# More filler matmuls on TensorE ahead of the first attention scores

## The chip, the cores and the metric

The kernel runs on one core of one Trainium2 chip. The metric is the device time of that core in microseconds. Each engine (TensorE or PE, VectorE or DVE, ScalarE or ACT, GpSimd or POOL) works through its own list of instructions in order and waits on semaphores for the others; SyncE (SP) and ScalarE also issue DMA transfers.

## The reference

One block of a conditioned transformer: a modulation vector from c, attention with 32 heads of 20, then a bilinear feed-forward, each with a layer norm ahead of it and a gated residual. x is 2048 rows of 640; all inputs are bf16.

```python
mod = (_silu(c) @ w_mod).reshape(c.shape[0], 6, 1, -1)
sa, ca, ga, sb, cb, gb = (mod[:, i].copy() for i in range(6))
h = _layernorm(x) * (1 + ca) + sa
qkv = (h @ wqkv) -> q, k, v, 32 heads of 20
o = softmax(q @ k^T * 20 ** -0.5) @ v
x = x + ga * (o @ wo)
h = _layernorm(x) * (1 + cb) + sb
x = x + gb * (((h @ w_gate) * (h @ w_up)) @ w_down)
```

(The lines are joined from the reference's functions.)

## The kernel before, in words

**Tiling.** The queries are cut into five chunks (512, 512, 512, 256, 256 rows). For each chunk the 32 heads are worked off in eight sets of four, one head to each strip of 32 rows of the array. Scores are computed transposed, keys on the partitions, in tiles of 128 x 512 (L1305); ScalarE takes the exponential of two or three tiles at once out of PSUM (L1341, 779 in all). About a fifth of the tiles (400 of 2048) go to VectorE instead, which builds the exponential from integer arithmetic: L1365 to bits, L1397 and L1405 split them, L1402 multiplies the halves. TensorE multiplies the result by V, extended by a column of ones that gives the softmax's denominator (L1831). After each chunk comes a suffix: output projection, residual, second layer norm (L1585 to L1592), transposes (L1603), gate and up products, and the down product (all recorded at L822 when they use the whole array, at L826 when cut into four strips of 32 columns).

**The head.** Up to the first scores this must happen: c is transposed on TensorE (L856), copied by VectorE (L854), passed through the sigmoid (L859 to L862); two blocks of 25 matmuls of one column each (L840) then give the modulation vectors ca and sa as soon as their weights have landed. Meanwhile VectorE and ScalarE compute the layer norm of the first 512 rows: tiles with even number by statistics on VectorE (L920, L925), odd ones by two passes with sums on ScalarE (L883, L886). Twenty transposes (L947) bring the rows into columns; the evictions (L955 on VectorE, L953 on ScalarE) apply the modulation and give hT. From it come the K projection of the first head set, the Q projection, and the K projection of the second set (L980, 20 matmuls each, cut into strips), whose evictions (L989, L990 for K, L994, L996 for Q) allow the first scores. The V products (L826, with wV) follow.

**What sets the order.** Nothing is ordered by hand. While it builds the program, the kernel simulates all engines with durations of its own (class Sched) and picks, whenever an engine is free in that simulation, a ready task by priority. The list of each engine that comes out is written into the program as it stands. An eviction can go to either of two engines: if ScalarE is idle in the simulation, it takes the eviction from VectorE's list (steal, L268). TensorE is served by pick_pe (L1981), which takes in turn: scores, other work when recent activity is low, products with V, other work, and last a filler.

**Fillers.** [...]the planner keeps a record of it: each matmul is entered with an area (a filler with 512, a full-array matmul with 2.37 for each nanosecond), and recent(t) sums the last 3413 ns. A filler (do_fill, L2088) multiplies the identity matrix with itself into a free PSUM bank; nothing reads it. Before the first scores it is one full-array matmul of 512 columns (L2100), later four strips (L2102). It is issued when nothing else is to be had, the simulated time is past a limit, and recent activity is below FILL_MIN:

```python
        if t > 4000 and fill_ok(t, fill_deps):
            return do_fill(t)
...
        return sc.recent(t) < FILL_MIN      # 4200
```

The same FILL_MIN also stands at L2038, where low activity lets other work go ahead of the products with V; that place is not touched. The simulated time starts at 700 ns and isn't the chip's time: the order that it leads to is fixed, the moments at which the chip reaches each instruction are not.

Of the kernel before, what the change touches and what calls it, by code (L numbers as in the profile page):

```python
# [464 lines left out]
GATE_F = [1.0, 0.869, 0.999, 0.673, 1.0]  # L465
FILL_MIN = 4200.0
FILL_HARD = 0.0
FILL_MODE = 'P'
DUP_MIN = 0.0
XN_POOL = ()  # L470
# [25 lines left out]
def build_kernel(nc, A_x, A_wqkv, A_wo, B_x, B_w_gate, B_w_up, B_w_down, c, w_mod, out):  # L496
# [14 lines left out]
    sc = Sched()  # L511
# [860 lines left out]
    for qi, (it, us) in enumerate(dquads):  # L1372
# [3 lines left out]
        def term(f, deps, dur, name, slot=None, src=None, last=False, it=it, qi=qi, st_=st_):  # L1376
            t = Task("dve", dur, f, deps, prio=(2.5 if not X_POOL else TPRIO) + .001 * qi, name=f"{name}.{qi}")
            t.lk = 1
            if slot is not None:
                t.acq = [(sSS, "s", 1)]  # L1380
            if slot is not None:
                tleft[it] = tleft.get(it, 0) + 1
            t.cond = lambda: it <= st_pv["item"] or (it == st_pv["item"] + 1 and tleft.get(it - 1, 0) == 0 and TAHEAD)

            def on_t(task):
                if slot is not None:
                    st_["ss"][slot] = task.slots["s"]
                    tleft[it] -= 1
                if last:
                    sB0.done(st_["slot"], task)  # L1390
                if src is not None:
                    st_["src"][src] = [task]
            t.on_start = on_t
            return sc.add(t)
# [14 lines left out]
        if X_POOL and qi % X_POOL == X_POOL - 1 and qi < len(dquads) - X_LAST and all(  # L1409
                dquads[z][0] == it for z in range(qi, min(len(dquads), qi + X_TAIL + 1))):  # L1410
            st_["xby"] = None
            for x in range(X_PIECES):
# [5 lines left out]
                t = Task("pool", w * POOL_NS + 180.0, fxp, [tm, te], prio=2.0 + .1 * qi + .01 * x, name=f"XP.{qi}")  # L1418
# [13 lines left out]
            t = term(fx, [tm, te], TT_2X, "X", src=0, last=True)  # L1432
# [320 lines left out]
    def mode_start(mode, t):  # L1753
        if sc.pe_mode is not None and sc.pe_mode != mode:
            return max(t, sc.pe_end + PE_SWITCH)
        return max(t, sc.pe_end)
# [224 lines left out]
    def pick_pe(t):  # L1981
# [56 lines left out]
        if sc.recent(t) < FILL_MIN and ring() >= RINGLOW and pick_x(t, True):  # L2038
            return True
        if sc.recent(t) < FILL_HARD and t > 20000 and do_fill(t):  # L2040
            return True
# [39 lines left out]
        if cands and not js and len(cands) >= 2 and (not PV0 or it >= PV0N or len(cands) >= PV0 or cands[0][0] == 'd'):  # L2081
            pv_issue(cands, t)
            return True
        if t > 4000 and fill_ok(t, fill_deps):
            return do_fill(t)
        return False

    def do_fill(t):  # L2088
        mode = FILL_MODE if pvstate["sidx"] else "X"
        start = mode_start(mode, t)  # L2090
        fs = G
        if pvstate["sidx"] == 0:
            fs = next((q for q in (GX, GC) if q.avail() is not None and q.avail()[0] <= t), GC)
        task = Task("pe", 216.0, ffill, fill_deps, ctr="pex", mode=mode, name="fill", acq=[(fs, "g", 1)])
        if not sc.acquire(task, t):
            return False
        b_ = task.slots["g"]
        idb = ident[:].unsqueeze(1).to_broadcast([128, 4, 128])
        if mode == "X":
            task.emits = [lambda e: e.matmul(ps[:, b_, :].rearrange("p (a b) -> p a b", a=4), ident[:], idb)]  # L2100
        else:
            task.emits = [lambda e, x=x: e.matmul(  # L2102
                ps[32 * x:32 * x + 32, b_, :].rearrange("p (a b) -> p a b", a=4), ident[:, 32 * x:32 * x + 32], idb,
                tile_position=(0, 32 * x), skip_group_check=True) for x in range(4)]
        sc.activity(start, 512.0)
        sc.left += 1
        sc.finish_issue(task, start, 216.0 * clk())
        fs.done(b_, task)
        sc.pe_mode = mode
        sc.pe_end = start + 216.0 * clk()  # L2110
        sc.free_at["pe"] = sc.pe_end
        sc.nfill += 1
        return True

    fill_deps = [p_id]
    ffill = None

    def fill_ok(t, fdeps):
        if any(d.done is None or d.done + SEM > t for d in fdeps):
            return False  # L2120
        if xcur[0] is not None:
            return False
        return sc.recent(t) < FILL_MIN

    just_s = [False]
    xcur = [None]
# [48 lines left out]
```

## Time and profile before

| | |
|---|---|
| time, median of 3 runs | 825.75 us (825.2 to 829.89) |
| span of the profiled execution | 824.0 us |
| mean granted TensorE clock | 0.996 |
| fillers before the first scores (L2100) | 14 |
| first scores (L1305) start | 18.33 us |
| first exponential (L1341) starts | 19.62 us |
| exponentials, all 779 | 757.2 us of ScalarE |
| last exponential ends | 788.2 us |

A busy TensorE in this profile means that some matmul was in its pipeline, not that it ran at full speed: ends are modelled, and neighbours overlap. Speed is read from the distance between the starts of equal matmuls, or from a group's time divided by its count, and the granted clock from its own column. DMA shares a little over 1 come from overlapping packets. A line number is that of the recording helper, so the tile names tell which product it is: hT with wk is a K projection, hT with wq a Q projection.

### The profile page before, as it was taken

How to read it: one execution, taken by the hardware profiler on the slowest of the kernel's cores; microseconds unless marked ns; L12 is line 12 of the kernel's file. 1: busy time of each engine (PE TensorE's matmuls, PEld its weight loads, DVE VectorE, ACT ScalarE, POOL GpSimd, SP SyncE). 2: the span in 40 equal slices, each digit the busy share in tenths (PEclk: the TensorE clock that was granted, in tenths of full speed). 3: DMA queues.
4: the chain of work that ended last, by engine and by line, in shares of the span. 5: the costliest groups of instructions: out<-in, count | busy, mean ns of one | idle time of the engine just before them, and what ended most of it. 6: DMA issues, size and time to landing. Idle time of an engine off the chain costs nothing.

```text
span 824.0 us, 27804 instructions
## 1 busy us (share of the span) xinstructions
PE 796.8 (97%) x11948; PEld 298.7 (36%) x11948; DVE 729.2 (88%) x1276; ACT 776.3 (94%) x822; POOL 70.9 (9%) x104
## 2 busy tenths in 40 slices
PE   8999999999999999999999999999999999999998
PEld 4433333322233222223332222233244443454577
DVE  6989999999899999999999999999689888758663
ACT  5899999899999999999999999999999999999931
POOL 2300000000011000000011000000011000001000
PEclk8999999999999999999999999999999999999999
DMA  9453311124400225000300222000300226205440
GB/s 295 124 166 79 89 51 35 36 71 114 117 17 24 57 66 163 22 6 22 74 30 13 52 49 52 5 15 26 86 4 13 56 66 133 48 29 113 108 89 19
DMA packets 115897, 54.26 MB, mean 66 GB/s; under 512 B 83771, under 2 KB 115775, under 8 KB 115775
## 3 DMA queue, kind: packets, MB, share of 16 engines
q1 hardware_dynamic: 114847, 51.33, 24.2%
q8 instruction: 95, 1.56, 0.8%
q10 hardware_dynamic: 928, 1.15, 0.4%
q14 instruction: 27, 0.22, 0.1%
HBM read 41.75 MB, written 8.41 MB: 61 GB/s over the span
## 4 chain that ended last, share of the span: by engine, by line
PE 50%; ACT 33%; DVE 9%; issue 7%; DMA 1%; ACTq 0%; DVEq 0%
ACT PP L1341 33%; PE ps_all L1305 16%; PE ps_all L826 14%; PE ps_all L1831 11%; DVE DB L1365 3%; PE ps_all L822 3%; PE ps_all L1032 3%; PE ps_all L980 2%; DVE DSS L1402 1%; DVE DSS L1405 1%; PE ps_all L947 1%; DVE DSS L1397 1%; DMA wm<-in_w_mod_dram 1%; DVE OT L1485 0%; PE ps_all L840 0%
## 5 line engine op out<-in xcount | busy, mean ns | idle before, releaser
L1341 ACT ACTIVATE PP<-ps_all 128x1024 bf16<-128x1024 f32 (+1 forms) x779 | 757.2, 1158 | 7.9 <-PE ps_all L1305 5.0
L1305 PE MATMUL ps_all<-QT,KT 32*128 32x512 bf16 (+1 forms) x2560 | 317.9, 340 | 16.7 <-ACT PP L1341 11.7
L1365 DVE TENSOR_SCALAR DB<-ps_all 128x512 int16<-128x512 f32 x400 | 264.9, 680 | 35.5 <-PE ps_all L1305 33.8
L1305 PEld LDWEIGHTS ps_all<-QT,KT 32*128 32x128 bf16 x2560 | 84.3, 91 | 279.5 <-ACT PP L1341 238.4
L1831 PE MATMUL ps_all<-PP,Vf 128*32 128x512 bf16 (+2 forms) x2080 | 162.9, 343 | 0.0
L1402 DVE TENSOR_TENSOR DSS<-DB,DSS 128x2048 bf16<-128x2048 bf16 x100 | 122.8, 1228 | 0.0
L826 PE MATMUL ps_all<-h2T,stg 128*32 128x512 bf16 x1440 | 113.9, 382 | 0.7 <-DVE DB L1365 0.4
L1490 POOL TENSOR_TENSOR OTn<-OT,invT 128x512 bf16<-128x512 f32 (+1 forms) x39 | 42.2, 1083 | 615.8 <-DVE invT L1488 615.8
L1831 PE MATMUL ps_all<-DSS,Vf 128*32 128x512 bf16 (+1 forms) x960 | 78.8, 347 | 0.4 <-DVE DSS L1405 0.3
L1831 PEld LDWEIGHTS ps_all<-PP,Vf 128*32 128x32 bf16 (+1 forms) x2080 | 46.9, 94 | 85.7 <-issue 79.7
L1397 DVE TENSOR_SCALAR DSS<-DB 128x2048 int16<-128x2048 int16 x100 | 70.2, 702 | 0.9
L1405 DVE TENSOR_SCALAR DSS<-DB 128x2048 int16<-128x2048 int16 x100 | 68.4, 684 | 1.1 <-PE ps_all L1831 1.1
L826 PE MATMUL ps_all<-wd,hprod 128*32 128x320 bf16 x1152 | 58.3, 301 | 0.1
L826 PEld LDWEIGHTS ps_all<-h2T,stg 128*32 128x32 bf16 x1440 | 31.1, 95 | 33.1 <-issue 19.8
L826 PEld LDWEIGHTS ps_all<-wd,hprod 128*32 128x32 bf16 x1152 | 27.5, 96 | 17.7 <-issue 9.9
L1831 PEld LDWEIGHTS ps_all<-DSS,Vf 128*32 128x32 bf16 x960 | 24.9, 95 | 22.2 <-issue 9.4
L826 PE MATMUL ps_all<-wo,Ocp 128*32 128x320 bf16 x560 | 30.9, 301 | 0.7 <-DVE DB L1365 0.4
L1678 DVE CAST gsb<-ps_all 128x512 bf16<-128x512 f32 (+1 forms) x46 | 28.6, 622 | 3.2 <-PE ps_all L826 3.1
L826 PE MATMUL ps_all<-wV,hT 128*32 128x320 bf16 x640 | 31.2, 301 | 0.0
L1485 DVE STREAM_TRANSPOSE OT<-ps_all 128x512 f32<-128x512 f32 (+1 forms) x40 | 24.2, 605 | 7.8 <-PE ps_all L1831 7.7
L1032 PE MATMUL ps_all<-hT,wq 128*32 128x512 bf16 x375 | 30.5, 382 | 0.0
L1689 DVE TENSOR_TENSOR hprod<-ps_all,gsb 128x512 bf16<-128x512 f32 x36 | 24.5, 680 | 4.9 <-PE ps_all L826 4.7
(124 smaller groups left out, 522.0 us busy)
## 6 DMA issues: line engine op xcount, KB each, us to landing
stg<-in_B_w_gate_dram SPq DMA_DIRECT2D x50, 160.0 KB
stg<-in_B_w_up_dram SPq DMA_DIRECT2D x50, 160.0 KB
QT<-q_rows SPq DMA_DIRECT2D x22, 128.0 KB
KT<-k_rows SPq DMA_DIRECT2D x84, 32.0 KB
wm<-in_w_mod_dram SPq DMA_DIRECT2D x3, 800.0 KB
x<-in_A_x_dram SPq DMA_DIRECT2D x7, 320.0 KB
xck<-in_A_x_dram SPq DMA_DIRECT2D x3, 640.0 KB
wd<-in_B_w_down_dram SPq DMA_DIRECT2D x1, 1920.0 KB
```

Source lines behind the costliest of these rows:

```text
L822: return lambda e, b: e.matmul(ps[:, b, c0:c0 + n], lhs(), rhs(), start=st, stop=sp)
L826: return lambda e, b: e.matmul(ps[32 * x:32 * x + 32, b, c0:c0 + n], lhs()[:, 32 * x:32 * x + 32], rhs(), tile_position=(0, 32 * x), start ...
L1032: f = [lambda e, b_, k=k, x=x: e.matmul(ps[x:x + min(32, w - x), b_, :], wx[:, k, r0 + x:r0 + min(x + 32, w)], hT[tc][:, k, :], tile_posit ...
L1305: ems.append(lambda e, i=i, kt=kt: e.matmul(dstf()[:, i * u.n:(i + 1) * u.n], KT[32 * u.s:32 * u.s + 32, u.j, kt * 128:(kt + 1) * 128], QT ...
L1341: return e.activation(PPs[g % 2][:, cellp["p"], 0:nu * 512], ps[:, b0:b0 + nu, :].rearrange("p b c -> p (b c)"), AFT.Exp, scale=ESCALE)
L1365: return e.tensor_scalar(DB0[:, st_["slot"], x * 512:(x + 1) * 512], bank(cell["b"]), EBIAS, 0.0, op0=ALU.add, op1=ALU.max)
L1397: return e.tensor_scalar(DSS[:, st_["ss"][0], :], DB0[:, st_["slot"], :], 0x7F, 0x3F00, op0=ALU.bitwise_and, op1=ALU.bitwise_or)
L1402: return e.tensor_tensor(d, DB0[:, st_["slot"], :].bitcast(BF16), d, ALU.mult)
L1405: return e.tensor_scalar(DSS[:, st_["ss"][1], :], DB0[:, st_["slot"], :], 0x7F80, 2, op0=ALU.bitwise_and, op1=ALU.bitwise_or)
L1490: f3 = lambda e: e.tensor_tensor(OTn[:, 0:n].rearrange("p (b c) -> p b c", c=32), OT[:, 0:n].rearrange("p (b c) -> p b c", c=32), invT[:, ...
L1678: f = lambda e: e.tensor_copy(gsb[:, gs, 0:n], ps[:, r.b["b"], 0:n])
L1831: ems.append(lambda e, i=i, kt=kt, stt=stt, stp=stp: e.matmul(ps[32 * s:32 * s + mc, BPV, 0:u.n], Vf[:, (kt * H + 4 * u.j + s) * VW:(kt * ...
```

## The change

Three constants are new. FILL_T0 replaces the fixed limit, so that fillers may begin at 2300 ns of simulated time instead of 4000, ahead of the transposition of c. Up to FILL_TH, 17000 ns, the activity below which a filler is issued is FILL_MINH, 6000, instead of 4200; the range takes in the head up to the first scores. The aim is to have TensorE's clock granted in full when the modulation products, transposes and first projections come.

```diff
 FILL_MIN = 4200.0
 FILL_HARD = 0.0
+FILL_T0, FILL_TH, FILL_MINH = 2300.0, 17000.0, 6000.0
 FILL_MODE = 'P'
...
-        if t > 4000 and fill_ok(t, fill_deps):
+        if t > FILL_T0 and fill_ok(t, fill_deps):
             return do_fill(t)
...
-        return sc.recent(t) < FILL_MIN
+        return sc.recent(t) < (FILL_MINH if t < FILL_TH else FILL_MIN)
```

The changed program has one line more, so its line numbers from L468 on are higher by one.

## The prediction

> **What bounds the kernel now.** I read the page's share of busy time, then the table of stretches, then the timeline of the head and of the tail. First the shares:
>
> ```profile
> PE 796.8 (97%) x11948; PEld 298.7 (36%) x11948; DVE 729.2 (88%) x1276; ACT 776.3 (94%) x822; POOL 70.9 (9%) x104
> ...
> PEclk8999999999999999999999999999999999999999
> ```
>
> Three engines look full, so the share decides nothing. The clock line is full in every slice but the first. By stage (columns: PE, PE weight load, DVE, ACT, POOL, clock, DMA share, GB/s):
>
> ```profile
> 10.00:13.00 3.00, 2.36 (x32) 2.10 (x29) 1.87 (x5) 1.82 (x3) 0.00 (x0) 0.50 1.10 331
> 13.00:15.10 2.10, 2.10 (x24) 0.75 (x26) 1.73 (x6) 0.94 (x3) 0.28 (x1) 0.50 1.14 298
> 15.10:17.20 2.10, 2.10 (x28) 0.82 (x24) 1.44 (x3) 1.15 (x4) 0.27 (x1) 0.60 1.07 363
> ...
> 28.00:50.00 22.00, 21.95 (x357) 10.09 (x349) 17.85 (x43) 18.13 (x22) 5.33 (x13) 1.00 0.52 164
> ...
> 200.00:400.00 200.00, 195.80 (x2477) 58.03 (x2477) 193.09 (x311) 199.19 (x216) 17.37 (x17) 1.00 0.21 56
> ...
> 800.00:824.00 24.00, 21.36 (x228) 17.92 (x220) 8.21 (x19) 4.46 (x12) 0.00 (x0) 1.00 0.07 22
> ```
>
> Three limits follow one another. Up to about 50 us TensorE's queue is the fullest (21.95 of 22). From 200 us on, ScalarE's exponentials are (199.19 of 200) until they end at 788.2. Then TensorE works off the feed-forward tail. A time saved in the head is kept only if it brings the exponentials forward. Half a clock is granted from about 10 to 17 us and nowhere else. The head on TensorE:
>
> ```profile
> 2.25 4.02 PE L2100 MATMUL ps_all<-ident 128*128 128x512 bf16 x9
> 7.91 0.78 PE L840 MATMUL ps_all<-scol,wm 128*128 128x1 bf16 x25 [1.65 <-DMA wm<-in_w_mod_dram]
> 8.55 1.02 PE L2100 MATMUL ps_all<-ident 128*128 128x512 bf16 x4
> 9.41 0.78 PE L840 MATMUL ps_all<-scol,wm 128*128 128x1 bf16 x25
> 10.05 2.29 PE L947 MATMUL ps_all<-ident,xn 128*128 128x128 bf16 x20
> 12.98 2.32 PE L980 MATMUL ps_all<-hT,wk 128*32 128x512 bf16 x20 [0.64 <-DVE hT L955]
> 15.09 2.09 PE L980 MATMUL ps_all<-hT,wq 128*32 128x512 bf16 x20
> 17.01 1.25 PE L980 MATMUL ps_all<-hT,wk 128*32 128x512 bf16 x20
> ```
>
> Nine fillers start 427 ns apart, so TensorE is at half speed until 6.27 although the clock column already says 1.00 (no change is on record yet). At 8.55 four fillers start 215 ns apart: full speed. The transposes again run at half speed, and so do the first K and Q projections, 2.1 us from start to start; the second K projection needs 1.08 us. The clock by half microseconds (0.96 in 9.5 to 10.0, 0.72 in 16.5 to 17.0) puts the fall at 9.96 and the return at 16.78, 6.82 us apart. What ScalarE does then:
>
> ```profile
> 18.32 0.58 ACT L990 CAST KT<-ps_all 128x512 bf16<-128x512 f32 x1 [2.06 <-PE ps_all L980]
> 18.80 0.83 ACT L886 ACTIVATE xn<-x,mv 128x640 bf16<-128x640 bf16 x1
> 19.53 0.19 ACT L886 ACTIVATION_READ_ACCUMULATOR xn<-x,mv 128x1 f32 x1
> 19.62 1.93 ACT L1341 ACTIVATE PP<-ps_all 128x1024 bf16<-128x1024 f32 x2
> ```
>
> The first scores start at 18.33, but the first exponential waits behind a K eviction and a layer-norm square until 19.62.
>
> [...]
>
> **The change part by part.** The order of instructions as built shows that the full-array fillers go from 14 to 24: 5 ahead of the transpose of c (was 1), 11 after it (was 9), 4 between the modulation products (unchanged), 4 new ones between the first transposes and the first K projection. The strip fillers later fall from 308 matmuls to 244 (77 rounds to 61). All other TensorE work is the same in kind and number, but the planner's simulated times move, so its greedy order changes from there to the end.
>
> 1. *Fillers ahead of c.* Start 1.51, five at 427: the transpose of c moves from 2.13 to about 3.65. Its consumer, the copy of c on VectorE, is queued behind statistics and starts only at 4.98. Cost 0.
>
> 2. *Eleven fillers.* From 3.77, cold to 6.55 (seven), then warm: end near 7.6. The modulation weights land at 7.9. Cost 0. [...]the end would be at most 3.77 + 11 x 0.427 = 8.47, 0.56 late.
>
> 3. *Clock.* [...]
>
> 4. *Transposes and evictions, warm.* Warm transposes at 24.71 us take 0.62 for 8, about 56 ns each, so 20 end near 11.35 instead of 12.34. Then evictions set the pace: three at 0.54 on VectorE from 10.44 end at 12.06, two at 0.82 on ScalarE from 10.67 end at 12.31. The K projection starts at 12.37 instead of 12.98: 0.6 gained.
>
> 5. *Four new fillers.* 11.35 + 4 x 0.215 = 12.2, hidden under these evictions. One waits for VectorE and one for ScalarE to free a bank, probably the early evictions (10.4 and 11.5). Queued behind them is the whole projection chain: cold, they would end at 12.34 + 1.71 = 14.05 and push it back 1.07.
>
> 6. *First K and Q projections.* Two times (2.1 - 1.08) = 2.0 gained. They end at 13.45 and 14.53. The Q weights landed by 12.85 (the transfer that waits for them was issued then), so DMA allows it; the V weights landed near 15.2, also in time.
>
> 7. *ScalarE ahead of the first exponential.* The Q eviction moves to ScalarE, behind 12.31 + 0.92 (sum), a square of 1.02 that waits for VectorE until 13.4, and another sum of 0.92: about 15.4 to 16.1. Scores 16.15, first exponential near 16.6, 3.0 earlier. But a square of 1.02 now follows it, where before it was ahead. Net 2.0. TensorE idles some 0.6 before these scores, so its chain gains the same 2.0. VectorE had barely any idle time in 17 to 28 us (2.36 of 2.40, 8.37 of 8.40), so part may be lost: range 0 to 3.0.
>
> 8. *Evictions on ScalarE.* Nineteen before and after, but two V and one hT come into the exponentials' stage and two K, of which one was ahead of it, and two late g go. After the first exponential, beside that square: 2.28 before, 3.34 after. Some 0.8 falls where ScalarE idled (0.36 + 0.39 near 28 us). I charge 0.5; range 0.3 to 1.1.
>
> 9. *Middle.* ScalarE's waits between first and last exponential sum to 8.3 (5.0 and 2.2 of exponentials, 1.1 of evictions). A new order can lose or gain some: 0, range -3 to +4. Fewer strip fillers gain nothing while ScalarE is the bound.
>
> 10. *Tail.* After the last scores before: 100 gate and up matmuls in strips and 16 of the split quad; now 40 and 0. Before, from the last exponential (788.17): output projection at +2.6, feed-forward of the last chunk (801.54) at +13.4. Now, with a 3.1 us down half first (88 x 0.035), projection at +3.55, ends +6.9, the other half +10.3, transposes and evictions 1.8 uncovered: +12.15. Gain 1.2, range 0 to 2.
>
> Sum: -2.0 + 0.5 + 0 - 1.2 = -2.7; 825.75 - 2.7 = 823.0.
>
> **Rivals.**
> - *Absorbed.* VectorE's layer norms and the weights' landings set the pace between 17 and 40 us (ScalarE waits 2.56 for scores at 39.72), the head gains nothing there and the tail's 1.2 is eaten by the extra evictions: 825. For it: VectorE full from 17 to 28. Against: its early idle (1.87 of 3.0, 1.73 of 2.1) lets it start sooner.
> - *Slower.* The new greedy order opens waits in the ScalarE stage, where before has nearly none to lose (0.9 in 200 to 600), or the clock stays down and fillers delay the projections by 1.1: +1 to +5, say 828. For it: 780 us of reordered work rest on durations that the planner assumes. Against: ScalarE has a ring of buffers ahead of it, and its list of exponentials is unchanged.
> - *Much faster.* The order also removes most of the 8.3 of waits: 823 - 6 = 817. Against: most lie before 60 us, where TensorE is full.
>
> **How the numbers follow.** Forecast (821 to 824.5) 0.5; absorbed 0.2; slower 0.25, of which 0.04 by over 1%; much faster 0.05, half of it past 1%. The predicted time is the forecast's. The range takes in the bounds of points 7 to 10 and most of the slower case: 819.5 to 828.5. One per cent is 8.3 us, which only the ends of two rivals reach, so within 1% has 0.93.
>
> **What would show it.** Right: clock at 1.00 from about 7 us on; first K projection near 12.4 and Q 1.08 later; first exponential near 16.6, a square behind it; last exponential near 786.7; the last chunk's gate products 12.2 after it. Wrong: clock 0.50 at 10 us or a late projection (points 3, 5); a head that gains but a last exponential at 788 or later (points 7 to 9); the tail no shorter (10).

## The result and the profile after

The changed kernel takes 822.48 us, the median of 6 runs (822.0 to 823.52); the kernel before, run beside it, 826.33 (6 runs, 825.2 to 829.89). The ratio is 0.9945, with a 95% interval of 0.9923 to 0.9968: faster by about half a per cent. The prediction was 823.0.

The page of the changed kernel, the same two rows as before:

```profile
PE 796.5 (97%) x11894; PEld 297.1 (36%) x11894; DVE 727.9 (89%) x1276; ACT 775.6 (95%) x822; POOL 71.7 (9%) x104
...
PEclk9999999999999999999999999999999999999999
```

The shares tell nothing again; the first slice of the clock row now reads full, although TensorE starts at half speed here too (the fillers start 427 ns apart up to 7.25 and 215 ns apart from 7.62; the first change of the clock is on record at 7.56). The same stretches (PE, weight load, DVE, ACT, POOL, clock, DMA share, GB/s):

```profile
10.00:13.00 3.00, 2.95 (x49) 1.95 (x49) 2.41 (x6) 2.16 (x4) 0.00 (x0) 1.00 1.10 332
13.00:15.10 2.10, 2.10 (x44) 1.20 (x40) 2.05 (x7) 1.90 (x5) 0.71 (x2) 1.00 1.14 298
15.10:17.20 2.10, 2.10 (x46) 0.85 (x34) 2.10 (x9) 1.61 (x3) 0.47 (x2) 1.00 1.07 363
```

From 10.0 to 17.2 us the clock is 1.00 where it was 0.50 to 0.60, and the three stretches count 139 matmuls where they counted 84 (one that spans a boundary counts in both). TensorE's busy time hardly tells them apart (7.15 against 6.56 of 7.2 us): the count shows the difference. The head on TensorE, whose lines stand one lower in the file than before:

```profile
1.51 2.31 PE L2101 MATMUL ps_all<-ident 128*128 128x512 bf16 x5 [1.51 <-POOL ident L780]
3.75 0.18 PE L857 MATMUL ps_all<-ident,c 5*128 5x5 bf16 x1
3.87 4.35 PE L2101 MATMUL ps_all<-ident 128*128 128x512 bf16 x11
8.06 0.77 PE L841 MATMUL ps_all<-scol,wm 128*128 128x1 bf16 x25
8.69 1.02 PE L2101 MATMUL ps_all<-ident 128*128 128x512 bf16 x4
...
10.18 1.28 PE L948 MATMUL ps_all<-ident,xn 128*128 128x128 bf16 x20
11.29 1.03 PE L2101 MATMUL ps_all<-ident 128*128 128x512 bf16 x4
12.36 1.26 PE L981 MATMUL ps_all<-hT,wk 128*32 128x512 bf16 x20
13.44 1.27 PE L981 MATMUL ps_all<-hT,wq 128*32 128x512 bf16 x20
```

Twenty transposes take 1.28 (before 2.29), and the K and Q projections start 1.08 apart (before 2.11). ScalarE around the first exponential:

```profile
13.20 0.83 ACT L887 ACTIVATE xn<-x,mv 128x640 bf16<-128x640 bf16 x1 [0.22 <-DVE mv L886]
...
14.75 0.69 ACT L997 ACTIVATE QT<-ps_all,qcol 128x512 bf16<-128x512 f32 x1
15.93 1.02 ACT L1342 ACTIVATE PP<-ps_all 128x1024 bf16<-128x1024 f32 x1 [0.49 <-PE ps_all L1306]
16.85 0.82 ACT L887 ACTIVATE xn<-x,mv 128x640 bf16<-128x640 bf16 x1
```

The square that stood ahead of the first exponential now stands behind it, at 16.85. And the tail, first of the kernel before, then after:

```profile
779.88 8.28 ACT L1341 ACTIVATE PP<-ps_all 128x1536 bf16<-128x1536 f32 x7
790.76 0.85 PE L822 MATMUL ps_all<-wo,Ocp 128*128 128x320 bf16 x5 [0.28 <-DVE OcT L1497]
794.12 3.44 PE L826 MATMUL ps_all<-wd,hprodt 128*32 128x320 bf16 x96
798.16 3.44 PE L826 MATMUL ps_all<-wd,hprodt 128*32 128x320 bf16 x96
801.54 11.09 PE L822 MATMUL ps_all<-h2Tc,stx 128*128 128x256 bf16 x100
```

```profile
777.16 8.35 ACT L1342 ACTIVATE PP<-ps_all 128x1536 bf16<-128x1536 f32 x7
786.13 3.16 PE L827 MATMUL ps_all<-wd,hprodt 128*32 128x320 bf16 x88
789.23 0.85 PE L823 MATMUL ps_all<-wo,Ocp 128*128 128x320 bf16 x5
792.59 3.44 PE L827 MATMUL ps_all<-wd,hprodt 128*32 128x320 bf16 x96
797.82 11.09 PE L823 MATMUL ps_all<-h2Tc,stx 128*128 128x256 bf16 x100 [1.12 <-ACT h2Tc L1611]
```

One half of the down product (3.16) now lies ahead of the output projection, and 1.12 us is left waiting before the gate products. They start 797.82 - 785.51 = 12.31 after the last exponential; before, 801.54 - 788.16 = 13.38.

So the two spans, 824.0 and 820.3, differ by three terms: the first exponential 19.62 to 15.93, **-3.69**; from its start to the end of the last one 768.54 to 769.58, **+1.04**; from there to the end 35.84 to 34.79, **-1.05**. The sum is -3.70.

### The profile page after: what moved, and what is told of

Same layout as the page of the kernel before. It is cut to its first block, busy times and chain, and to the rows that moved or that the text cites. A ratio compares the mean times of both kernels' runs of the same rounds, so it can differ in the third digit from the quotient of the medians.

```text
span 820.3 us, 27666 instructions
## 1 busy us (share of the span) xinstructions
PE 796.5 (97%) x11894; PEld 297.1 (36%) x11894; DVE 727.9 (89%) x1276; ACT 775.6 (95%) x822; POOL 71.7 (9%) x104
## 4 chain that ended last, share of the span: by engine, by line
PE 42%; ACT 35%; DVE 14%; issue 7%; DMA 1%; SPq 0%; POOL 0%; ACTq 0%; DVEq 0%; POOLq 0%
ACT PP L1342 35%; PE ps_all L1306 13%; PE ps_all L827 13%; PE ps_all L1832 9%; DVE DB L1366 5%; PE ps_all L823 3%; PE ps_all L1033 2%; DVE DSS L1403 1%; DVE DSS L1398 1%; DVE DSS L1406 1%; PE ps_all L2101 1%; DVE st L921 1%; PE ps_all L981 1%; DVE wd L1294 1%; DVE hprod L1690 0%
## 5 line engine op out<-in xcount | busy, mean ns | idle before, releaser
L827 PE MATMUL ps_all<-h2T,stg 128*32 128x512 bf16 x1440 | 116.0, 382 | 1.1 <-DVE DB L1366 0.4
L1491 POOL TENSOR_TENSOR OTn<-OT,invT 128x512 bf16<-128x512 f32 (+1 forms) x39 | 39.7, 1017 | 617.6 <-DVE invT L1489 617.6
L1498 DVE STREAM_TRANSPOSE OcT<-OTn 128x512 bf16<-128x512 bf16 (+1 forms) x40 | 23.8, 596 | 2.2 <-POOL OTn L1491 2.2
```

The source lines that it names most:

```text
L827: return lambda e, b: e.matmul(ps[32 * x:32 * x + 32, b, c0:c0 + n], lhs()[:, 32 * x:32 * x + 32], rhs(), tile_position=(0, 32 * x), start ...
L1491: f3 = lambda e: e.tensor_tensor(OTn[:, 0:n].rearrange("p (b c) -> p b c", c=32), OT[:, 0:n].rearrange("p (b c) -> p b c", c=32), invT[:, ...
```

## The experiments

My theory at this point: the head's fillers keep the clock up and thereby bring the exponentials forward one to one, and the tail's microsecond comes from the new order alone. The rivals: the order does it all and the fillers are idle decoration; or the fillers cost as much as they bring. Each change of one constant reorders the whole program, so the parts had to be separated at the point where instructions are written out: a helper `HEADF(i)` says how often the i-th filler of the head is emitted, while the planner's simulation, and with it the order of everything else, stays as it was.

```diff
+def HEADF(i):
+    return 0 if i in (1, 2, 3, 4, 14, 15) or 20 <= i <= 23 else 1
...
-            task.emits = [lambda e: e.matmul(ps[:, b_, :].rearrange("p (a b) -> p a b", a=4), ident[:], idb)]
+            task.emits = [lambda e: e.matmul(ps[:, b_, :].rearrange("p (a b) -> p a b", a=4), ident[:], idb)] * HEADF(sc.nfill)
```

This is the order alone: 14 head fillers as before, everything else as after (the 61 rounds of strip fillers too). The others of the first set: the changed kernel once more, unedited; the order of before with the changed kernel's 24 fillers (the same helper gives `5 if i == 0 else 3 if i == 9 else 1`, and a group of four is put in behind the first transposes); the order of after with no head filler at all (`return 0`).

> The changed kernel once more, as the yardstick of this set: 822.5, at every run within 1 us of it. First exponential at 15.9 us, last one ending at 785.5. A theory that the gain was one lucky pair of runs would have it within 1 us of the kernel before.

> The order of the kernel before on all engines, with only the changed kernel's ten extra head fillers put into TensorE's list (4 ahead of the transposition of c, 2 ahead of the modulation products, 4 after the first transposes). Theory 'clock': first K projection at 12.4, first exponential near 17 (K eviction and square still ahead of it), 2 to 2.6 us of gain kept to the end: 823 to 824. Theory 'order': the head's 2 us are absorbed by VectorE and the landings, no gain without the new order: 825.5 to 826.5.

> The changed kernel's order on all engines, with the ten extra head fillers left out when the program is written. Theory 'clock': clock falls to one half near 10 us, first K and Q projections 2.1 us each, first exponential 2.5 to 3 us later than 15.9; only the tail's 1 us is left of the gain: 824.5 to 826. Theory 'order': no loss, 822.5. In both the runs should spread over several us as those of the kernel before do[...].

> The changed kernel's order with all 24 head fillers left out. Theory 'clock': half speed from the first matmul until 16 to 17 us, first exponential at 18.5 to 20, 826 to 828, with little spread[...]. Theory 'order': 822.5 to 823.5.

| kernel | median us (range, runs) | ratio to before [95%] | span | first exponential | last one ends | from there to the end |
|---|---|---|---|---|---|---|
| before | 826.56 (824.59-830.25, 60) | | 824.0 | 19.62 | 788.16 | 35.8 |
| after, again | 822.35 (821.39-822.9, 6) | 0.9948 [0.9927, 0.9969] | 819.3 | 15.94 | 784.54 | 34.8 |
| fillers only | 824.8 (823.38-828.92, 22) | 0.9991 [0.9977, 1.0006] | 821.9 | 17.18 | 785.69 | 36.2 |
| order only | 824.72 (822.52-826.79, 22) | 0.9977 [0.9965, 0.9989] | 824.4 | 19.31 | 789.65 | 34.8 |
| order, no head fillers | 824.05 (823.28-825.02, 21) | 0.9964 [0.9953, 0.9975] | 822.2 | 18.88 | 787.44 | 34.8 |

(Before's times are from this set, its profile is the one shown above. The time is longer than the span, by some 1.8 us in the two kernels with the old order and 2.1 in those with the new one; compare each column with itself.)

Three things follow. The tail belongs to the order: 34.8 in all three kernels that have it, 36.2 in the one that has only the fillers. The head belongs to the fillers, and most of it passes through: between no head fillers and all of them the first exponential moves by 2.94, and in this pair of profiles the end of the last one by 2.90, the span by 2.9. The pair flatters the change, though: the medians of the two kernels differ by 1.7, and against the changed kernel's first profile (last exponential ending at 785.51) the end moves by only 1.9. Exponential by exponential, the 2.94 has shrunk to 2.4 by 28 us. And the two parts together bring 4.2 in the medians, 1.8 for each alone (the interval of the fillers alone still takes in 1). The surplus of 0.6 is smaller than these intervals, some 1 us to each side, so it may be nothing; but the profiles show two things that work that way, one at the head and one further on.

With the fillers alone the projections run at full speed, in the old order too:

```profile
12.27 1.26 PE L985 MATMUL ps_all<-hT,wk 128*32 128x512 bf16 x20
13.35 1.27 PE L985 MATMUL ps_all<-hT,wq 128*32 128x512 bf16 x20
```

But fillers can also cost. The order alone, on TensorE:

```profile
8.55 1.87 PE L2106 MATMUL ps_all<-ident 128*128 128x512 bf16 x4
10.21 0.85 PE L846 MATMUL ps_all<-scol,wm 128*128 128x1 bf16 x25
10.92 2.29 PE L953 MATMUL ps_all<-ident,xn 128*128 128x128 bf16 x20
14.01 2.32 PE L986 MATMUL ps_all<-hT,wk 128*32 128x512 bf16 x20 [0.80 <-DVE hT L961]
```

The same with no head filler:

```profile
9.38 0.81 PE L846 MATMUL ps_all<-scol,wm 128*128 128x1 bf16 x25 [0.70 <-DVE xn L900]
10.04 2.29 PE L953 MATMUL ps_all<-ident,xn 128*128 128x128 bf16 x20
13.14 2.32 PE L986 MATMUL ps_all<-hT,wk 128*32 128x512 bf16 x20 [0.80 <-DVE hT L961]
```

In both TensorE is at half speed: twenty transposes take 2.29, and K and Q start 2.09 and 2.08 apart (the clock column reads 1.00 there all the same). Four fillers at 427 ns each stand in a gap that holds four at 215 ns: they push the second modulation product from 9.38 to 10.21 and the K projection from 13.14 to 14.01. In this profile the fillers at half speed are worse than none, which is one reason why leaving out all 24 cost less than I had expected (824.05 instead of 826 to 828). They may not run so in every execution (an estimate from the times): runs of the order alone go down to 822.52, which the kernel without fillers never reached (823.28 at best). The order alone also lost the clock later, at 79.0 us:

```profile
75.60:79.00 3.40, 2.67 (x48) 1.17 (x46) 3.37 (x6) 3.08 (x4) 0.00 (x0) 1.00 0.22 58
79.00:82.40 3.40, 3.40 (x28) 0.64 (x25) 1.54 (x4) 2.05 (x2) 0.00 (x0) 0.50 0.22 71
```

Twenty-eight matmuls are counted where 48 were, and ScalarE has work for 2.05 instead of 3.08: its last exponential ends 2.2 later than with no head filler, of which 0.43 comes from the head and 1.8 from after it.

**Which fillers matter.** Second set, edits of the changed kernel with its order kept: the last four fillers left out (`return 0 if 20 <= i <= 23 else 1`); the six early ones left out (`return 0 if i in (1, 2, 3, 4, 14, 15) else 1`). A third one tests whether ScalarE's queue ahead of the Q eviction sets the first exponential, by taking one layer-norm tile from it (this one reorders):

```diff
-LN_ACT = [1, 3, 5, 7]
+LN_ACT = [1, 3, 7]
```

> The changed kernel's order without the four fillers between the first transposes and the first K projection. Theory 'transposes count' (transposes keep the clock up as other matmuls do): [...]the clock stays up, K projection at 12.4, 822.4. Theory 'transposes do not count': [...]the clock falls before the K and Q projections in some runs, which then take 2.1 us each: median 823 to 824.5, spread of 2 us and more.

> The changed kernel's order without the four fillers ahead of the transposition of c and without two of the eleven after it, so that TensorE is idle from 6.3 to 7.9 us as before. Theory 'early fillers matter': [...]the four cold fillers between the modulation products delay the second product and the four behind the transposes delay the K projection by 1 us: 824 to 826, spread 3 to 4 us. Theory 'the last four are enough': 822.5 to 823.

> The changed kernel with the layer norm of row tile 5 on VectorE instead of ScalarE, everything planned anew. ScalarE has 1.9 us less ahead of the first exponential (a sum and a square), so that the eviction of Q no longer waits behind them: first exponential at 15.6 instead of 15.9, VectorE 1 us more before 20 us. 821 to 822.5 if ScalarE is what holds the head now; 823 to 824 if VectorE is.

> A second profile of the old order with the extra head fillers, whose times fell into two groups, 823.4 to 825.4 at a mean clock of 0.998 to 1.000 and 827.2 to 828.9 at 0.993 to 0.996. If this one falls into the upper group, a stretch of half clock of some 10 us is expected after the head, most probably where activity is lowest, at the second set of modulation products near 65 to 80 us; if it falls into the lower group, no fall of the clock at all.

Without the last four: 821.87 us (821.57 to 822.43, 6 runs), ratio 0.9929 [0.9902, 0.9956], indistinguishable from the changed kernel. The projections still run at full speed (K and Q start 1.07 apart), from 12.57 (0.2 later), so these four fillers aren't needed. Without the early six: 823.75 (822.57 to 826.67, 22 runs), ratio 0.9959 [0.9946, 0.9972], and in the profile

```profile
9.03 1.87 PE L2106 MATMUL ps_all<-ident 128*128 128x512 bf16 x4
...
13.49 1.37 PE L2106 MATMUL ps_all<-ident 128*128 128x512 bf16 x4
14.79 1.26 PE L986 MATMUL ps_all<-hT,wk 128*32 128x512 bf16 x20
```

the fillers between the products are at half speed (1.87 for four), the last four too at first (1.37), and K starts 2.43 late; the first exponential is at 18.36. This profile is of one of the longest runs (826.35), and the head isn't all of it: from the first to the last exponential it takes 771.08 us where the changed kernel's two profiles took 769.58 and 768.60. Its matmuls run at full speed there, but at 100 us the scores wait for rows of Q that were written out and are read back, and ScalarE waits with them:

```profile
100.33 0.40 PE L1311 MATMUL ps_all<-QT,KT 32*128 32x512 bf16 x4 [1.65 <-DMA QT<-q_rows]
100.77 2.97 ACT L1347 ACTIVATE PP<-ps_all 128x1024 bf16<-128x1024 f32 x3 [1.53 <-PE ps_all L1311]
```

So what the six early fillers are worth is better read from the times of this set. The median of the runs without them is 1.9 us above that of the kernel without the last four, and their fastest (822.57) is slower than the slowest there (822.43). The six early fillers carry most of the change's gain in the head. With one layer-norm tile less on ScalarE the median is 821.9 (820.61 to 824.74, 6 runs), 0.9932 [0.9905, 0.9959]; the first exponential stays at 15.97, because the Q eviction doesn't move (14.79 against 14.75), now waiting for the Q projection itself: I had named the wrong work ahead of it. This kernel, planned anew, has lost the tail's microsecond (35.86 from the last exponential to the end). The second profile of fillers only gave 823.47 and no fall of the clock. Of that kernel's 22 runs 13 lie about 823.8, and 9 between 827.16 and 828.92, these with a mean clock of 0.993 to 0.996.

**A second fall of the clock.** The kernel before spreads likewise: of its 117 runs in these sets, 48 lie above 827.2 (median 829.54), the others have a median of 825.71. In the profile shown in the prediction the clock falls only in the head. So something else can happen later. A measure of TensorE's work: add up the matmuls that start in 3.41 us (in that profile the time from the rise of the clock on record at 6.54 to its fall at 9.96), each by columns times its part of the array, and divide by what full-array matmuls of 512 columns would fill at 215 ns each. By this area share the lowest stretch after the head in that profile starts at 66.4 us, with 0.26, where the 50 one-column products of a later modulation block lie. Test: four full-width fillers ahead of each block of 25, in the block's own bank, added to the fillers-only kernel. And the kernel before, unedited, was profiled twice more.

```diff
+        if v >= 2:
+            t0 = r.tasks[0]
+            f0 = t0.emits[0]
...
+            ff = lambda e: e.matmul(ps[:, r.b["b"], :].rearrange("p (a b) -> p a b", a=4), ident[:], idb4)
+            t0.emits = [ff] * 4 + [f0]
```

> The old order with the extra head fillers, and besides four full-array fillers ahead of each of the two later blocks of 25 one-column modulation products (near 64 to 68 us[...]). They add 8 x 0.215 = 1.7 us to TensorE there. Theory 'second fall': the upper group of times (827.2 to 828.9, clock 0.993 to 0.996) comes from the clock falling in this stretch and is gone: all runs between 823.5 and 826. Theory 'elsewhere' (the low stretch near 751 us, or the head): the upper group stays with about four runs in ten, at 828 and more.

> The kernel before, profiled once more. Of its runs so far some four in ten took 827.2 to 830.3 at a mean clock of 0.989 to 0.994. If this one is among them: half clock in the head and again from near 70 us for about 10 us (theory 'second fall'), or half clock near 755 us (theory 'elsewhere'). If not: half clock in the head alone.

> The same as the other look at the kernel before, for a second chance at a run with a low clock.

With them: 825.46 us (824.85 to 826.88, 14 runs), ratio 0.9988 [0.9974, 1.0002]. The group above 827 is gone; the lowest runs lie about 1.5 higher, near what eight full-width fillers cost (8 x 0.215 = 1.7). Four of the 14 runs, at 826.3 to 826.88, still show a mean clock of 0.998 where the others, up to 826.08, show 1.00. A fall of 3.4 us, as long as the one near 758 below, would give 0.998 (3.4 x 0.5 / 824 = 0.002), so a fall is probably left (an estimate; none of the four was profiled). The other low stretch, near 752 us, had no fillers added. The second new profile of before (one run, 828.62) caught the fall itself, in the stretches

```profile
64.80:68.20 3.40, 3.40 (x70) 2.02 (x66) 3.33 (x8) 3.40 (x5) 0.00 (x0) 1.00 0.26 86
68.20:75.00 6.80, 6.80 (x54) 1.49 (x51) 4.88 (x9) 4.75 (x5) 0.00 (x0) 0.50 0.19 52
...
757.70:761.10 3.40, 3.40 (x56) 1.57 (x51) 3.04 (x5) 3.04 (x3) 0.00 (x0) 0.50 0.49 109
```

TensorE is busy for 3.40 of 3.40 ahead of the fall and the clock falls all the same, for 6.8 us; ScalarE then has work for 4.75 of those 6.8. What TensorE does in the stretch before it:

```profile
64.92 0.58 PE L840 MATMUL ps_all<-scol,wm 128*128 128x1 bf16 x17
...
66.74 0.47 PE L840 MATMUL ps_all<-scol,wm 128*128 128x1 bf16 x10
...
67.50 0.63 PE L840 MATMUL ps_all<-scol,wm 128*128 128x1 bf16 x19
```

Forty-six of the 50 one-column matmuls stand in these three rows: they keep TensorE busy and use one column each, so that the area share of this stretch comes to 0.31. In that profile the first exponential starts at 17.88 and the last ends at 790.63: 772.75 us against 768.54, 4.2 more, with two falls in it. The first new profile (828.19, mean clock 0.998) has a first exponential at 20.39 and takes 770.07 from there to the last. Compared with the profile of before in the prediction, exponential by exponential, the fall near 68 costs 2.9 us in the second, and the place near 758 costs 1.2 in each of the two. The speed of before's head differs as well: in the second new profile, the one in the prediction and the first new one, the four fillers between the modulation products take 1.02, 1.02 and 1.87, K and Q start 1.52, 2.11 and 2.11 apart, and the first exponential starts at 17.88, 19.62 and 20.39.

Last, the two edits that looked best, no last four and one layer-norm tile less, in one kernel:

> The changed kernel without the four fillers behind the transposes and with row tile 5's layer norm on VectorE: the two variants that were not slower than the change, together. Neither effect lies on the path by itself, so 821.5 to 822.3, a difference from the changed kernel that cannot be told from none; 821 or less if the two add up.

822.13 us (820.82 to 823.39, 6 runs), ratio 0.9936 [0.9914, 0.9958]. They don't add: the tail is again 35.85, and the profiled run has a mean clock of 0.998. No kernel here beats the change by more than the runs differ.

## Why the prediction was right, and where its sizes were off

It forecast 2.7 us less, from half a clock in the head and a rearranged tail. Both happened, and the medians moved by 3.85, the profiled spans by 3.7. That the time itself came within 0.5 of 823.0 is partly luck: before's median, from three runs, stood 0.6 below that of six. By its points:

- **1 and 2, fillers ahead of c and after it: right.** c is transposed at 3.75 (3.65 forecast) and nobody waits. The eleven fillers end near 8.05, since the clock's rise is on record at 7.56, later than the 6.55 that I had carried over from before's profile (6.54 on record there); the modulation product starts 0.15 later, inside the bound of 0.56. The moment differs from profile to profile and can't be carried over: the eleven take 4.35 us here, 3.67 in the changed kernel's second profile, 4.02 without the last four, 2.85 in fillers only.
- **3, the clock: right, on an estimate.** It stays up, 1.00 from 10.0 to 17.2 us. That the added fillers would be enough was my estimate, and how much work the clock needs, and over what time, isn't shown. The profiles show single stretches: in before the 3.41 us from 6.54 have an area share of 0.26 and the clock falls at 9.96; in the changed kernel the 3.41 us from 7.56 have 0.62 and no fall follows. But before's 0.26 from 66.4 us was followed by no fall in the same profile (the clock reads 1.00 from 66 to 82), while in the second new one it fell after 0.31.
- **4 and 6, transposes and projections: right to 0.02.** K at 12.36 (12.37), Q at 13.44 (13.45), K of the second set at 14.52 (14.53).
- **5, four new fillers: hidden, but of no use.** The run without them shows it: K and Q start 1.07 apart, at full speed. I counted them because I took transposes to do less for the clock than other matmuls, which was my estimate; no run supports it. In the changed kernel the 3.41 us from 21.21 have an area share of 0.49 with their 19 transposes and 0.19 without, and the clock reads 1.00 from 21.2 to 28.0. How much a transpose counts stays open.
- **7, ScalarE ahead of the first exponential: the mis-sized term.** Forecast 16.6, measured 15.93. The square that waits for VectorE started at 13.20, not 13.4, and the passes take 0.83 and 0.72 from start to start, not 1.02 and 0.92, since the read of the sum overlaps the next instruction (it runs from 13.94 to 14.13, the next starts at 14.03): 13.20 + 0.83 + 0.72 puts the Q eviction at 14.75 instead of 15.4 or later. The square behind the exponential costs 0.82 by the same count, not 1.02 (18.80 to 19.62 before), so the net gain is 3.69 - 0.82 = 2.9, where the sum had 2.0. Fillers only reaches 17.18 with nearly the same K projection (12.27): so 1.25 of the 3.69 is the order ahead of the first exponential, and 0.83 of that is the square changing sides.
- **8 and 9, evictions and middle: +0.5 was forecast beyond the square.** From first to last exponential the profile pair gives +1.04, the changed kernel's second profile (784.54 - 15.94 = 768.60) only +0.06. Less the square's 0.82, that leaves +0.2 and -0.8. The two profiles of the changed kernel part at two places, by 0.24 near 75.6 us and by 0.7 near 96, with the clock up in both: the scores come later there, at 75.4 after a wait for rows of K that are read back (0.22). That most of the second place is such a wait too is likely, since the run without the early six waits 1.65 for Q there, but not shown. Why the evictions' 2.28 to 3.34 doesn't appear in the second profile stays open.
- **10, tail: right.** 1.05 to 1.07 against 1.2, and the run with the order alone shows that it is the order's.

The sum of its terms was -2.0 + 0.5 - 1.2 = -2.7. In the prediction's own terms the two profiles give -2.9 (head, less the square), +0.2 or -0.8 (evictions and middle), and -1.05 (tail): -3.7 and -4.7.

One statement was wrong: that the clock is down "from about 10 to 17 and nowhere else". It held for the one profile in hand. The kernel before can lose the clock again near 68 us (0.50 for 6.8 us, 2.9 us lost) and near 758 us (0.50 for 3.4 us, 1.2 us lost). The 12 runs of the changed kernel lie within 2.1 us (821.39 to 823.52), before's 60 of the first set within 5.7, and all 12 show a mean clock of 1.00. Its page's clock row has no slice below 9. Its order spreads the 50 one-column products out, first before, then after:

```profile
L840 PE MATMUL ps_all<-scol,wm x50: 163/163/178, 66.7 to 70.2; 128*128 128x1 bf16 x50
```

```profile
L841 PE MATMUL ps_all<-scol,wm x50: 163/163/178, 67.2 to 73.6; 128*128 128x1 bf16 x50
```

They start within 3.5 us before and within 6.4 us after. The least area share of any 3.41 us near there rises from 0.26 to 0.38. Near 752 us it rises too, from 0.32 to 0.46. No constant of the change aims at either. That the higher area shares keep the clock up is my estimate: no run moved only these products. It fits the surplus of the two halves together: the order alone loses at the head what the fillers gain, and the fillers alone still have slow runs (9 of 22 above 827, at a mean clock of 0.993 to 0.996). And the order isn't immune: with its fillers cut, it lost the clock at 79.0, after 3.40 us in which TensorE was busy for 2.67.

The rivals: *absorbed* fell in the main, but not wholly: of the head's 2.9 between no fillers and all of them, 1.7 to 2.9 came out at the end. *Slower* had one true part, fillers at half speed delay the projections (by 0.87, in order only), but in the changed kernel they don't. *Much faster* had no support: from first to last exponential no profile takes less than 768.1 us (before 768.54).

## What to carry to other kernels

Judge a filler by the speed at which it and the work behind it run: here sixteen early ones, nearly back to back from 1.51 us, were followed by a full clock in the head (four more in 1.02, K and Q 1.08 apart), while four that ran at half speed (1.87) stood in the way of the work (K 0.87 later). Look for stretches with a busy TensorE and little array area, such as one-column products in a row: after one with an area share of 0.31 the clock was 0.50 for 6.8 us, and four wide matmuls ahead of each block of 25 left no run above 827. When one kernel's runs spread by half a per cent, take several profiles before explaining a difference of that size from one pair.

## What the runs showed of the hardware that was not expected

- A busy TensorE doesn't hold the clock: 3.40 of 3.40 us busy at 64.8 to 68.2 in the second new profile of before, area share 0.31, and the clock was 0.50 for the next 6.8 us.
- The clock stays up through transposes: without the four fillers behind them TensorE is busy for 1.93 of the 3.00 us from 10.0, 20 of its 44 matmuls there are transposes, and the clock reads 1.00; K and Q then start 1.07 apart.
- The clock column can read 1.00 although the spacing shows half speed: in before the fillers start 427 ns apart up to 5.63 (215 at 8.55) in a stretch that reads 1.00; in the order alone K and Q start 2.09 apart under 1.00; the profiled run without the early six has a mean clock of 1.00 and four fillers in 1.87 (1.02 at full speed). Spacing is the surer sign.
